# Block sums of the weights moved into attention chunks, a second pair with two levels in its first layer, rectifications on ScalarE and a padded state

## The chip, the cores and the metric

The kernel runs on one core of a Trainium2 chip. Its engines are TensorE (PE, with its weight load PEld), VectorE (DVE), ScalarE (ACT), GpSimd (POOL) and SyncE (SP), which issues most transfers. The metric is the device time of one execution in microseconds. A time before or after is the median of several executions. The profile is one further execution.

## The reference

The first half is linear attention with decay, for 4 batches, 8 heads, 768 positions and 64 columns per head. Positions go in blocks, and a 64x64 state per head carries the past:

```
intra = ((q_b k_b^T) * Dmask) v_b
inter = (q_b * lam_pow) kv_state
out_b = intra + inter
kv_state = lam_block * kv_state + (k_b * rev_pow)^T v_b
```

Its output, with the heads side by side, is x (4 batches x 768 x 512). The second half mixes x by a Fourier transform over positions and columns and adds a two-layer network:

```
u  = x + real(fft(fft(x, axis=1), axis=2))
un = (u - mean(u)) / sqrt(var(u) + 1e-6)
y  = u + max(un @ w_ch1, 0) @ w_ch2       # w_ch1: 512 x 2048, w_ch2: 2048 x 512
```

All of it is in float32. The two weights come in as 64-bit floats and are converted on the chip.

## The kernel before, in words

**Front.** Each batch b goes through six attention chunks of 128 positions. `attn_in` loads k, q and v of a chunk (L263, on SP's queue, two buffers each), multiplies k by the decay on GpSimd (L270), transposes k and q on TensorE (L274, L279) and copies them out on ScalarE (L276, L281). `attn_out` makes the scores (L298), scales them by the decay on VectorE (L302), makes the state's increment (L315), takes the state on (L319 on GpSimd multiplies by the decay, L320 on VectorE adds the increment), and then sums two products into one bank: the old state with the scaled queries (L328, one 64x64 product per head) and the scores with v (L332). ScalarE copies the result (L335), and TensorE turns it back (L348). State tiles alternate: `st[0]`, `st[1]`. Batch 0 keeps its mirrored rows on the chip (`TURNED`); the others send theirs through DRAM and gather them with GpSimd's indirect transfers (L439 to L452). After that comes the transform (`fft_ln`, L516 to L611) and the normalization.

Twelve groups of 256 rows come out, (b, g). The first four (`PLAIN`) go through the plain network `mlp` (L635 first layer, L649 second layer, rows stored from `y`, L660 to L661), in between the attention and transform work of later batches: `weave` and `beside` mix generators by planned costs, which each `yield` gives. The weights are loaded and converted between them (`load_weights`, L209 to L225; buffers tagged "e", two of them, which the transposed rows L576 use too).

**Late.** The other eight groups (`LATE`) are taken in four pairs of 2 x 256 rows. A pair's two layers are done by a fast matrix product with seven block products in place of eight (`PRODUCTS`). The second layer of every pair, and both layers of pairs 3 and 4, apply that twice (`deep_first`, L967; `deep_second`, L1037): 7 x 7 products of blocks with 128 moving columns. The first layer of pairs 1 and 2 applies it once (`first_layer`, L882): in eight steps i, each with 14 matmuls of 256 columns into three banks X, Y and Z. `DEEP = 2` says how many pairs do so. In a step TensorE writes and adds to bank X several times, and ScalarE reads X between (L904, L911, L914), so the next addition waits for that copy. VectorE adds Y or Z to what ScalarE has copied (L906, L894, L915) and rectifies it in place (L907, L895, L916); `finish` of a step, which runs in the next step, also rectifies X on ScalarE into `sv` (L892) and makes the sums L896 and L897.

Two levels need block sums of the weights (four sums for each of seven blocks of each weight). `keep_sums` (L714) makes those of the second weights during the first layer of pair 1, `keep_sums_w` (L731) those of the first weights during that of pair 2, both on GpSimd with tiles tagged "tx" (six buffers), and SP stores each in DRAM. Before a block product, three of them are loaded again (`load_three`, L755). The fourth is written over a quarter of the weight: by GpSimd in place for the second weights (L718), by a load for the first (`place_sums_w`, L741).

**What sets the order.** Each engine works through its own list in order. A scheduler that places instructions by planned costs makes the list from the program; instructions in `tc.keep_in_program_order` keep their place. SP's list holds stores and loads alike: each waits for its semaphore in its turn.

Of the kernel before, what the change touches and what calls it, by code (L numbers as in the profile page):

```python
# [10 lines left out]
F32 = mybir.dt.float32  # L11
# [65 lines left out]
def kernel(  # L77
# [97 lines left out]

    st = [const.tile([128, HP, D], F32, name=f"st{i}") for i in range(2)]

# [75 lines left out]

    ins, oTs, eo = {}, {}, {}
    LEADS = (0,)
# [3 lines left out]
    def attn_in(b, c):  # L259
# [13 lines left out]
        for hp in range(HP):  # L273
            nc.tensor.transpose(ptk[:, hp, :], pair(kt, hp), ident)  # L274
        kT = new(at, [128, HP, C], "kT", bufs=2)
        nc.scalar.copy(kT, ptk)  # L276
        ptq = psum_a([128, HP, C])
        for hp in range(HP):
            nc.tensor.transpose(ptq[:, hp, :], pair(qt, hp), ident)  # L279
        qT = new(at, [128, HP, C], "qT", bufs=2)  # L280
        nc.scalar.copy(qT, ptq)  # L281
# [7 lines left out]
    def attn_out(b, c, head):  # L289
# [14 lines left out]
        if last and b - 1 in LEADS:  # L304
            mirror_a(b, pin=True)
        yield 1.5


        s_old, s_new = st[(c + 1) % 2], st[c % 2]
        if not last:  # L310
            pu = psum_a([128, HP, D])
            for hp in range(HP):
                for hi in range(2):
                    h = 2 * hp + hi
                    mm(pu[HD[hi], hp, :], lhsT=kd[:, h, :], rhs=vt[:, h, :], start=True, stop=True)  # L315
            if c == 0:
                nc.vector.tensor_copy(s_new, pu)
            else:
                nc.gpsimd.tensor_tensor(s_new, s_old, spow.broadcast_to([128, HP, D]), op=ALU.mult)  # L319
                nc.vector.tensor_tensor(s_new, s_new, pu, op=ALU.add)  # L320
            yield 0.9


        po = psum_a([128, HP, C])
        if c > 0:
            for hp in range(HP):
                for hi in range(2):
                    mm(po[HD[hi], hp, :], lhsT=s_old[HD[hi], hp, :], rhs=qs[HD[hi], hp, :],  # L328
                       start=(hp == 0), stop=False, skip_group_check=True)
        for hp in range(HP):  # L330
            for hi in range(2):
                mm(po[HD[hi], hp, :], lhsT=vt[:, 2 * hp + hi, :], rhs=sc[hi][:, hp, :],  # L332
# [9 lines left out]
        yield 2.0  # L342
        yield from head

        def turn(oT):
# [364 lines left out]

    s2.td = []
    s2.begun = wt.tile([128, 1], F32, name="begun")

    def keep_sums(k):  # L714

        pin = tc.keep_in_program_order
        B11, B12, B21, B22 = quarters_b(s2.B[PRODUCTS[k][1]])
        pin(nc.gpsimd.tensor_tensor(B12, B22, B12, op=SUB))  # L718
        T1, T2, T4 = t = [new(s2.yp, [128, HF // 2, HM // 2], "tx", bufs=6) for _ in range(3)]
        s2.td.append([dram.tile([128, HF // 2, HM // 2], F32, name=f"td{k}{i}") for i in range(3)])  # L720
        for i, o, x, y, op in ((1, T2, B12, B11, ADD), (0, T1, B22, T2, SUB), (2, T4, B21, T2, SUB)):
            pin(nc.gpsimd.tensor_tensor(o, x, y, op=op))
            nc.sync.dma_start(s2.td[k][i], o)

    s2.sd = []

# [3 lines left out]

    def keep_sums_w(k):  # L731

        pin = tc.keep_in_program_order
        A11, A12, A21, A22 = quarters_w(s2.A[PRODUCTS[k][0]])
        S3, S2, S1, S4 = [new(s2.yp, [128, FH // 2], "tx", bufs=6) for _ in range(4)]
        s2.sd.append([dram.tile([128, FH // 2], F32, name=f"sd{k}{i}") for i in range(4)])
        for i, o, x, y, op in ((3, S3, A11, A21, SUB), (1, S2, A22, S3, SUB), (0, S1, S2, A11, ADD), (2, S4, A12, S2, SUB)):
            pin(nc.gpsimd.tensor_tensor(o, x, y, op=op))
            nc.sync.dma_start(s2.sd[k][i], o)

# [25 lines left out]
    PAIRS = len(LATE) // 2  # L766
    DEEP = 2
    pairs = [Pair() for _ in range(PAIRS)]
# [106 lines left out]
    def first_layer(j):  # L875
# [12 lines left out]
        def finish(i, X, Z):  # L888
# [5 lines left out]
            V.tensor_tensor(a12, two(Z), a12, op=ADD)  # L894
            V.tensor_scalar(a12, a12, 0.0, None, op0=ALU.max)  # L895
            V.tensor_tensor(s1, a21, a22, op=ADD)  # L896
# [3 lines left out]
        for i in range(HF):  # L900
# [5 lines left out]
            V.tensor_tensor(a11, two(Y), a11, op=ADD)  # L906
            V.tensor_scalar(a11, a11, 0.0, None, op0=ALU.max)  # L907
            if last:
# [6 lines left out]
            V.tensor_tensor(a22, two(Z), a22, op=ADD)  # L915
            V.tensor_scalar(a22, a22, 0.0, None, op0=ALU.max)  # L916
            last = (i, X, Z)
            if j < min(DEEP, 2) and i < len(PRODUCTS):
                if i == 0:
                    tc.keep_in_program_order(nc.gpsimd.tensor_copy(s2.begun, h["a11"][:, 0, 0, 0:1]))  # L920
                (keep_sums, keep_sums_w)[j](i)
            if i == HF - 3:
# [216 lines left out]
    def late():  # L1139
        for j in range(PAIRS):  # L1140
            if j < DEEP:
                open_pair(j)
                if j == 0:
                    run(inputs(0))
                first_layer(j)
                if j + 1 < DEEP:
                    in_step(second_layer(j) + [(inputs(j + 1), iter(()))])
        in_step(second_layer(DEEP - 1) + [w for j in range(DEEP, PAIRS) for w in deep_pair(j)])
# [31 lines left out]
    def run(gen):  # L1180
        return sum(gen)
# [82 lines left out]
```

## Time and profile before

| | us |
|---|---|
| median of 3 executions (796.07 to 801.15) | 797.12 |
| profiled execution | 798.86 |
| its span, first to last instruction | 796.9 |
| TensorE busy | 766.8 (96%) |
| VectorE busy | 587.7 (74%) |
| ScalarE busy | 216.7 (27%) |
| GpSimd busy | 195.6 (25%) |
| first layer of pair 1, L882 | 428.7 to 478.6 |
| first layer of pair 2, L882 | 521.7 to 570.8 |
| first layer of pair 3, L967, begins | 611.2 |

A line of the profile names the line of the kernel, the engine, the operation, and what is written from what with sizes and number. In a time line the first column is the start and the second the duration, in us from the start of the span; in brackets is the idle time ahead of the instruction and what ended it. "SPq" is a transfer issued by SP. Each matrix product in float32 appears as two matmuls. A matmul's duration is longer than its distance to the next, because they overlap; distances are what counts.

### The profile page before, as it was taken

The page shows a single profiled execution, that of the slowest core. Times are in us where ns is not written, and L with a number is a line of the kernel's source. Part 1 is how long each engine was busy: PE and PEld are TensorE (multiplying, and loading weights), DVE is VectorE, ACT ScalarE, POOL GpSimd, SP SyncE. Part 2 cuts the span into 40 slices and gives each one's busy share as a digit, 9 for nine tenths or more (in the row PEclk, how much of TensorE's full clock was granted, in tenths as well). Part 3 has the DMA queues.
Part 4 walks back from the last instruction along what each step waited for, and adds up shares of the span by engine and source line. Part 5 has one row for each costly group of instructions (what it writes and reads, how often), then busy time and mean ns, then how long its engine had stood idle before and what let it go on. Part 6 is the DMA issues. An engine that isn't in the chain of part 4 may idle for free.

```text
span 796.9 us, 14576 instructions
## 1 busy us (share of the span) xinstructions
PE 766.8 (96%) x5616; PEld 647.2 (81%) x5616; DVE 587.7 (74%) x1148; ACT 216.7 (27%) x512; POOL 195.6 (25%) x196
## 2 busy tenths in 40 slices
PE   6989999999999999999999999999999999999996
PEld 5768776858675766777956889998999999999995
DVE  6899889685853573246598998769977699758983
ACT  3755443324431221221200221012210442024300
POOL 3233231011101020121003960279204101230021
PEclk9999999999999999999999999999999999999999
DMA  9979624238842037443232375345954555455432
GB/s 241 260 152 253 179 84 130 92 58 215 206 131 87 27 79 144 103 132 106 47 71 89 138 239 170 95 167 190 326 170 145 165 175 178 129 177 187 125 121 79
DMA packets 152331, 116.80 MB, mean 147 GB/s; under 512 B 113998, under 2 KB 113998, under 8 KB 152262
## 3 DMA queue, kind: packets, MB, share of 16 engines
q1 hardware_dynamic: 147120, 103.39, 46.1%
q0 software_dynamic: 2112, 6.69, 2.5%
q10 hardware_dynamic: 3030, 5.78, 2.1%
q8 instruction: 45, 0.74, 0.4%
q14 instruction: 24, 0.20, 0.1%
HBM read 83.58 MB, written 32.25 MB: 145 GB/s over the span
## 4 chain that ended last, share of the span: by engine, by line
PE 77%; DVE 10%; DMA 6%; issue 4%; ACT 2%; POOL 1%; SPq 0%; POOLq 0%; ACTq 0%; DVEq 0%
PE p L1037 21%; PE p L882 12%; PE p L967 11%; PE pm L649 9%; PE pm L635 8%; PE pa L516 3%; PE pa L332 3%; PE pa L298 3%; DMA raw<-in_moe_w_ch_dram 2%; DMA x<-xb,ix 2%; PE pa L328 2%; PE pa L274 1%; PE pa L315 1%; PE pa L348 1%; PE pa L279 1%
## 5 line engine op out<-in xcount | busy, mean ns | idle before, releaser
L635 PE MATMUL pm<-ut,w 128*128 128x256 f32 x512 | 118.8, 381 | 0.0
L649 PE MATMUL pm<-w,hr 128*128 128x512 f32 x256 | 115.7, 596 | 0.1
L635 PEld LDWEIGHTS pm<-ut,w 128*128 128x128 f32 x512 | 94.5, 190 | 14.0 <-issue 2.1
L649 PEld LDWEIGHTS pm<-w,hr 128*128 128x128 f32 x256 | 46.6, 190 | 49.3 <-issue 48.0
L1051 POOL TENSOR_TENSOR y<-y,u 128x512 f32<-128x512 f32 x12 | 18.8, 1570 | 199.1 <-DVE y L1060 156.7
L1037 PE MATMUL p<-tx,sx 128*128 128x128 f32 x416 | 54.9, 275 | 0.0
L1037 PEld LDWEIGHTS p<-tx,sx 128*128 128x128 f32 x416 | 50.6, 192 | 0.0
L882 PE MATMUL p<-ur,w 128*128 128x256 f32 x192 | 46.9, 379 | 0.1
L270 POOL TENSOR_TENSOR kd<-k,decay 128x512 f32<-128x512 f32 x20 | 22.2, 1109 | 95.9 <-PE pa L315 58.0
L1045 DVE TENSOR_TENSOR y<-p,y 128x128 f32<-128x128 f32 x92 | 25.6, 286 | 22.4 <-PE p L1037 15.7
L1043 ACT COPY y<-p 128x128 f32<-128x128 f32 x48 | 12.8, 266 | 104.1 <-PE p L1037 103.8
L882 PEld LDWEIGHTS p<-ur,w 128*128 128x128 f32 x192 | 36.3, 190 | 5.7 <-issue 0.5
L302 DVE TENSOR_TENSOR sc<-pa,decay 128x512 f32<-128x512 f32 x48 | 31.5, 683 | 8.5 <-PE pa L298 8.2
L1037 PE MATMUL p<-w,ha 128*128 128x128 f32 x288 | 37.4, 275 | 0.0
L298 PEld LDWEIGHTS pa<-qT,kT 64*128 64x128 f32 x384 | 26.0, 193 | 13.2 <-ACT qT L281 7.2
L1037 PEld LDWEIGHTS p<-w,ha 128*128 128x128 f32 x288 | 35.0, 192 | 0.2
L332 PE MATMUL pa<-sc,v 128*64 128x128 f32 x384 | 31.5, 282 | 3.8 <-DVE sc L302 3.7
L643 ACT ACTIVATE hr<-pm 128x256 f32<-128x256 f32 x44 | 16.7, 384 | 65.9 <-PE pm L635 65.6
L298 PE MATMUL pa<-qT,kT 64*128 64x128 f32 x384 | 30.7, 292 | 3.2 <-ACT qT L281 2.9
L549 POOL TENSOR_SCALAR ve<-mv 128x2 f32<-128x2 f32 x12 | 3.4, 286 | 122.6 <-DVE mv L546 122.6
L882 PE MATMUL p<-sx,w1s 128*128 128x256 f32 x128 | 32.9, 380 | 0.2 <-DVE sx L785 0.2
L332 PEld LDWEIGHTS pa<-sc,v 128*64 128x64 f32 x384 | 23.1, 137 | 11.4 <-DVE sc L302 5.3
(227 smaller groups left out, 1717.4 us busy)
## 6 DMA issues: line engine op xcount, KB each, us to landing
tx<-td SPq DMA_DIRECT2D x84, 256.0 KB, 2.9
raw<-in_moe_w_ch_dram SPq DMA_DIRECT2D x32, 512.0 KB, 5.4
tx<-sd SPq DMA_DIRECT2D x42, 256.0 KB, 2.7
sd<-tx SPq DMA_DIRECT2D x28, 256.0 KB, 2.0
k<-in_k_dram SPq DMA_DIRECT2D x24, 256.0 KB, 5.0
q<-in_q_dram SPq DMA_DIRECT2D x24, 256.0 KB, 6.0
v<-in_v_dram SPq DMA_DIRECT2D x24, 256.0 KB, 4.4
td<-tx SPq DMA_DIRECT2D x21, 256.0 KB, 2.0
```

Of the source, the lines that this page charges most:

```text
L270: nc.gpsimd.tensor_tensor(kd, kt, kpow, op=ALU.mult)
L298: mm(pss[hi][:, hp, :], lhsT=kT[HD[hi], hp, :], rhs=qT[HD[hi], hp, :], start=True, stop=True)
L302: nc.vector.tensor_tensor(t, pss[hi], decay[:, hi::2, :], op=ALU.mult)
L332: mm(po[HD[hi], hp, :], lhsT=vt[:, 2 * hp + hi, :], rhs=sc[hi][:, hp, :], start=(c == 0 and hp == 0), stop=(hp == HP - 1), skip_group_chec ...
L516: mm = nc.tensor.matmul(ps[:, n, :], lhsT=piece(a, i, n), rhs=cs[0:rows, a, i in (2, 3), n, :], start=(a == 0), stop=(a == 1))
L635: nc.tensor.matmul(ps, lhsT=w1[:, c, 128 * fc:128 * fc + 128], rhs=ut[:, c, :], start=(c == 0), stop=(c == KO - 1))
L649: nc.tensor.matmul(ps, lhsT=hr[(fc - f0) // 4][:, fc % 4, 128 * i:128 * i + 128], rhs=w2[:, fc, :], start=(fc == f0), stop=(fc == f1 - 1))
L882: nc.tensor.matmul(ps, lhsT=s2.A[a][:, kt, 128 * i:128 * i + 128], rhs=U[b][:, kt, :], start=(first and kt == 0), stop=(kt == 1), skip_gro ...
L967: nc.tensor.matmul(ps[:, 128 * i:128 * i + 128], lhsT=ab[m][0][:, 128 * i:128 * i + 128], rhs=ab[m][1], start=(start and i == 0), stop=Tru ...
L1037: nc.tensor.matmul(ps[:, 0:HM // 2], lhsT=ab[m][0][i], rhs=ab[m][1][:, i, :], start=(start and i == 0), stop=(i == HF // 2 - 1), skip_grou ...
L1045: V.tensor_tensor(o, ps[:, 0:HM // 2], o, op=ADD)
L1051: nc.gpsimd.tensor_tensor(o, y, u, op=ADD)
```

## The change

- The first layer of pair 2 has two levels like pairs 3 and 4 (`DEEP = 1`), so only pair 1 uses `first_layer`.
- Block sums of six weight blocks (24 sums) are made on GpSimd in the first four attention chunks of batches 2 and 3, three in each, in buffers "e" and a new one "ss". Each is stored by SP. The remaining 32 are made during the first layer of pair 1, and three quarters of the second weights are loaded back at its start (`place_sums_b`).
- In that layer the three rectifications after VectorE's additions are made by ScalarE.
- In batches 2 and 3 ("padded") the state is updated in place in one tile, and ScalarE copies it into a tile with zeros in the other head's rows; L328 multiplies all 128 rows. The increment, state and score products follow each other without a point at which other work may be put between. Zeros are set at each batch's start.
- `kT` and `qT` have one buffer in place of two.

```diff
-    st = [const.tile([128, HP, D], F32, name=f"st{i}") for i in range(2)]
+    st = const.tile([128, HP, D], F32, name="st")
+    sd = const.tile([128, HP, 2, D], F32, name="sd")
+    turns_of = [st, sd[:, 0:HP // 2].rearrange("p h a d -> p (h a) d")]
...
-        kT = new(at, [128, HP, C], "kT", bufs=2)
+        kT = new(at, [128, HP, C], "kT")
...
-        yield 1.5
-        s_old, s_new = st[(c + 1) % 2], st[c % 2]
+        padded = b not in TURNED and b - 1 not in LEADS
+        yield 2.4 if padded and not last else 1.5
+        s_old, s_new = (st, st) if padded else (turns_of[(c + 1) % 2], turns_of[c % 2])
+        if padded and c == 0:
+            nc.gpsimd.memset(sd, 0.0)
...
-            yield 0.9
+            if not padded:
+                yield 0.9
...
-                    mm(po[HD[hi], hp, :], lhsT=s_old[HD[hi], hp, :], rhs=qs[HD[hi], hp, :],
-                       start=(hp == 0), stop=False, skip_group_check=True)
+                    old, qh = (sd[:, hp, hi, :], qs[:, hp, :]) if padded else (s_old[HD[hi], hp, :], qs[HD[hi], hp, :])
+                    mm(po[HD[hi], hp, :], lhsT=old, rhs=qh, start=(hp == 0), stop=False, skip_group_check=True)
+        if padded and not last:
+            for hi in range(2):
+                nc.scalar.copy(sd[HD[hi], :, hi, :], st[HD[hi]])
         for hp in range(HP):
-            for hi in range(2):
+            for hi in (1, 0) if padded else (0, 1):
...
         yield from head
+        if padded and c < 4:
+            if not sums:
+                sums.append(early_sums())
+            run(part(sums[0], 3.0))
...
-    def keep_sums(k):
-    def keep_sums_w(k):
+    def block_sums(layer, k, quarters, shape, stage):
+        Q11, Q12, Q21, Q22 = quarters
+        S3, S2, S1, S4 = [stage[i](shape) if callable(stage[i]) else stage[i] for i in range(4)]
+        d = (s2.sd, s2.td)[layer][k] = [dram.tile(shape, F32, name=f"{'st'[layer]}d{k}{i}") for i in range(4)]
+        if layer == 0:
+            todo = ((3, S3, Q11, Q21, SUB), (1, S2, Q22, S3, SUB), (0, S1, S2, Q11, ADD), (2, S4, Q12, S2, SUB))
+        else:
+            todo = ((3, S3, Q22, Q12, SUB), (1, S2, S3, Q11, ADD), (0, S1, Q22, S2, SUB), (2, S4, Q21, S2, SUB))
+        for i, o, x, y, op in todo:
+            tc.keep_in_program_order(nc.gpsimd.tensor_tensor(o, x, y, op=op))
+            if o is not Q12:
+                nc.sync.dma_start(d[i], o)
+            yield 1.0
+    def early_sums():
+        k1, k2, f1, f2 = slice(0, 2), slice(2, 4), slice(0, FH), slice(FH, DFF)
+        b1, b2, c1, c2 = slice(0, HF), slice(HF, FO), slice(0, HM), slice(HM, DM)
+        blocks = [(0, 0, w1[:, k1, f1]), (1, 0, w2[:, b1, c1]), (0, 1, w1[:, k2, f1]), (1, 1, w2[:, b2, c1]),
+                  (0, 5, w1[:, k2, f2]), (1, 6, w2[:, b2, c2])]
+        for layer, k, t in blocks:
+            for d in block_sums(layer, k, (quarters_w, quarters_b)[layer](t), SHAPES[layer],
+                                [lambda s: new(ep, s, "e")] + [ep.tile(SHAPES[layer], F32, tag="ss", bufs=1, name=f"ss{layer}{k}")]
+                                + 2 * [lambda s: new(ep, s, "e")]):
+                yield d
+    def later_sums(i):
+        for layer, k in (((1, 3),), ((1, 2),), ((1, 4),), ((1, 5),), ((0, 3),), ((0, 4),), ((0, 2), (0, 6)))[i]:
+            q = (quarters_w, quarters_b)[layer]((s2.A, s2.B)[layer][PRODUCTS[k][layer]])
+            run(block_sums(layer, k, q, SHAPES[layer], [q[1] if layer else stage_tx] + 3 * [stage_tx]))
+    def place_sums_b():
+        for k in (0, 1, 6):
+            nc.sync.dma_start(quarters_b(s2.B[PRODUCTS[k][1]])[1], s2.td[k][3])
...
-    DEEP = 2
+    DEEP = 1
...
-            V.tensor_scalar(a12, a12, 0.0, None, op0=ALU.max)
+            nc.scalar.activation(a12, a12, AF.Relu)
...
-            V.tensor_scalar(a11, a11, 0.0, None, op0=ALU.max)
+            nc.scalar.activation(a11, a11, AF.Relu)
...
-            V.tensor_scalar(a22, a22, 0.0, None, op0=ALU.max)
+            nc.scalar.activation(a22, a22, AF.Relu)
...
-                (keep_sums, keep_sums_w)[j](i)
+                later_sums(i)
...
     def late():
-        for j in range(PAIRS):
-            if j < DEEP:
-                open_pair(j)
-                if j == 0:
-                    run(inputs(0))
-                first_layer(j)
-                if j + 1 < DEEP:
-                    in_step(second_layer(j) + [(inputs(j + 1), iter(()))])
+        open_pair(0)
+        run(inputs(0))
+        first_layer(0)
         in_step(second_layer(DEEP - 1) + [w for j in range(DEEP, PAIRS) for w in deep_pair(j)])
```

## The prediction

> **What bounds the kernel now.** I read the page first, busy shares and the 40 slices, then the chain that ended last, then the time line of the three stages that the diff touches.
>
> ```profile
> PE 766.8 (96%) x5616; PEld 647.2 (81%) x5616; DVE 587.7 (74%) x1148; ACT 216.7 (27%) x512; POOL 195.6 (25%) x196
> PE   6989999999999999999999999999999999999996
> PE 77%; DVE 10%; DMA 6%; issue 4%; ACT 2%; POOL 1%; SPq 0%; POOLq 0%; ACTq 0%; DVEq 0%
> ```
>
> TensorE is the bound from the third slice to the end, at full clock. The reader is to see what follows: matmul time taken out anywhere after about 60 us comes off the end, and so does any new wait of TensorE count in full. GpSimd and ScalarE have three quarters of the span free, but on average only; what matters is who waits for them in the two places where they get work.
>
> The first place is the first pair's first layer (428.7 to 478.6 us), one of its eight steps:
>
> ```profile
> 452.09 2.61 POOL L722 TENSOR_TENSOR tx<-w2s,tx 128x512 f32<-128x512 f32 x2
> ...
> 453.67 1.03 PE L882 MATMUL p<-ur,w1s 128*128 128x256 f32 x4
> 453.94 0.91 DVE L916 TENSOR_SCALAR ha<-ha 128x256 f32<-128x256 f32 x1
> 454.53 1.03 PE L882 MATMUL p<-sx,w 128*128 128x256 f32 x4
> ...
> 454.78 0.38 ACT L892 ACTIVATE sv<-p 128x256 f32<-128x256 f32 x1 [1.40 <-PE p L882]
> ...
> 456.06 0.41 DVE L896 TENSOR_TENSOR hs<-sv,ha 128x256 f32<-128x256 f32 x1
> ...
> 456.39 1.48 DVE L897 TENSOR_TENSOR hs<-ha,sv 128x256 f32<-128x256 f32 x1
> 456.46 0.37 ACT L911 COPY ha<-p 128x256 f32<-128x256 f32 x1 [1.29 <-PE p L882]
> ...
> 457.12 1.03 PE L882 MATMUL p<-sx,w1s 128*128 128x256 f32 x4
> ...
> 457.80 0.41 DVE L894 TENSOR_TENSOR ha<-p,ha 128x256 f32<-128x256 f32 x1
> ```
>
> Groups of four matmuls follow each other every 0.864 us without a gap. The group at 457.12 may start only after the copy L911 has read the bank, and L911 starts 0.2 us after its matmuls because ScalarE has nothing in front of it. VectorE is behind (L894 is 2.4 us after its matmuls), but nobody on TensorE waits for it. L897 takes 1.48 us here and 0.42 us once GpSimd is idle.
>
> The second place is the queue that loads attention chunks of batch 3:
>
> ```profile
> 312.34 0.39 SPq L263 DMA_DIRECT2D k<-in_k_dram  x1
> ...
> 315.02 0.85 SPq L263 DMA_DIRECT2D k<-in_k_dram  x1
> ...
> 329.95 0.37 SPq L263 DMA_DIRECT2D k<-in_k_dram  x1
> 330.66 0.37 SPq L263 DMA_DIRECT2D q<-in_q_dram  x1
> 335.72 0.37 SPq L263 DMA_DIRECT2D v<-in_v_dram  x1
> 336.33 0.38 SPq L263 DMA_DIRECT2D k<-in_k_dram  x1
> ```
>
> These are keys of chunks 2, 3, 4 and 5; their transposes run at 328.7, 335.6, 341.7 and 347.8 us, so each load is 11 to 20 us ahead, of which 4 are the transfer. Chunks follow every 6.07 us there.
>
> [...] The trace shows 0.17 us of idle weight load ahead of L332 after L328 and again after L332. [...]
>
> **The change, part by part.** The sum is made against the profiled execution (798.86 us, span 796.9, so about 2.0 around it); it is 1.7 above the median of 797.12, and I apply the difference to the median.
>
> *Second pair's first layer two-level.* Removed: 7 products x 8 x 2 = 112 matmuls, 224 in the trace, at 0.864/4 = 0.216 us: 48.4 us (521.67 to 570.75 less 0.67 us of second layer). Added: 7 x 7 x 4 = 196, 392 in the trace. In the later pairs eight take 0.893 us (784 in 611.17 to 698.72), so 43.8 us. **-4.6 us** on TensorE. The VectorE and GpSimd work that comes with it, and 21 loads of 256 KB more, are what pairs 3 and 4 have now behind an unbroken TensorE; the DMA share there is 0.45 to 0.6. I cost it at nothing, 0 to +3 if the loads of sums, the seven replaced quarters and the next inputs (34 loads of 256 KB and two of 512 KB in 44 us, some 220 GB/s, against 390 seen at 570 us) come late.
>
> *Padded state, batches 2 and 3.* The eight L328 matmuls of a chunk become 128 rows deep with 64 columns, as L332's. L332's sixteen take 1.03 us, L328's 1.02: no price in themselves. Two changes of mode per chunk go (state update to L328, L328 to L332), 0.17 us each at most, in 10 chunks, and where matmuls of the MLP now stand between the state update and L328 or inside L332 (six places) one interruption of 0.2 us. Between 0 and 3.4 + 1.2 = 4.6; I take **-3 us**. The ScalarE copies into the padded tile (20 of 64x256, some 0.38 us by L352) are queued ahead of the copy of the output, behind VectorE's state sum; a next use is 5 us later, so nothing.
>
> *24 sums in attention.* Three per chunk in four chunks of both batches, 128x512, 1.06 us by L270 alone, 1.3 with VectorE beside them, in GpSimd's order ahead of some key products (L270) and state products (L319); and 24 stores on SP's queue, each of which waits for its sum, ahead of the k, q and v loads of the next chunks. Two sums share two buffers with the weight conversion, so stores must land (2.0 us) before reuse.
> Batch 3: the order puts a sum behind the indirect output store, which starts at 327.74 now (VectorE's y). Then: three sums to 332, key product, key load of chunk 3 issued at 332.5 instead of 315, lands 336.5, its use is at 337.5 (more MLP is ordered ahead): just hidden. Key product 3 to 337.6, two sums to 340.2, key load 4 issued 340.5, lands 344.5 against 344.2; the query load is one sum later, 346.4 against 344.9: 1.5 us. Key product 4 to 345.6, three sums to 349.5, key load 5 lands 353.8 against 351.9: 2 us. With 4.4 us for a load, as the median is over both batches, some **+5 us** (0 where the loads land in 3.2 us and VectorE's y comes earlier; +10 where the two batches' chunks go at 9 instead of 6 us).
> Batch 2: chunks are 9 to 17 us apart, and the loads keep 1 to 3 us of their slack: **+1** (0 to +5).
>
> *Sums in the first pair's first layer.* 32 instead of 28, at 38.75/28 = 1.38 us: GpSimd is busy until 477.4 instead of 471.8. Three quarters of the second weights come back by loads at the layer's start, for products 45 us later. The second layer's loads follow the last sums; nothing, unless that layer starts on time (then +1).
>
> *Rectifications on ScalarE.* 24 leave VectorE (0.91 us each with GpSimd beside it), which is not waited for: no gain. [...] In its order the rectification of a12 of step i-1 stands **ahead of** the copy L911 of step i, and it waits for the VectorE sum L894, which stands behind L896 and L897. So TensorE's 457.12 group now waits for: end of s4 group (0), L892 to 0.63, L896 from 0.67 with a mean wait of half a GpSimd sum (0.65) and 0.41, L897 1.40 more (it meets the next sum), L894 0.34, rectification 0.45, copy and handover 0.36: 4.3 us, where three groups give 2.59. **1.7 us per step** (1.0 to 2.4). Steps become 7.75 us; from 436.4 on, 5.5 of seven meet GpSimd: 9.4, and 0.16 to 0.5 in the rest where the splits come in: **+10 us**. Bounds: 0 if VectorE gets in between sums, 14.
>
> Sum: -4.6 - 3 + 5 + 1 + 10 = +8.4; span 805.3, profiled 807.3, median **805.5 us**.
>
> **Rivals.**
> 1. *The rectification chain does not hold TensorE* (not slower). Place: ScalarE's copy L911. It decides from L896 and L897 together below 1.1 us after L892; uncontended they take 0.8. Against it: 1.48 for L897 in nearly all of the 16 steps. Then +8.4 - 10 = -1.6: 795.5; with the attention loads hidden too, -7.6: 789.5.
> 2. *The loads in attention stay hidden*: for it, GpSimd is a quarter busy; against it, stores with waits stand ahead of the loads in one queue. +2.4: 799.5.
> 3. *The queue locks both batches*: conversion buffers, stores and loads wait for each other in batch 2 as well, 2 to 3 us in each of eight chunks, some +18 in place of +6: 817.
> That the two-level layer isn't faster can't be: both prices are in the trace.
>
> **How the numbers follow.** The forecast (800 to 811) 0.50, of which a bit over half is slower by over 1% (8 us, about what a measurement of this kernel can tell from no change); rival 1 alone 0.16 and with both gains 0.08; rival 2 0.11; rival 3 0.15. Slower 0.29 + 0.15 = 0.44, and 0.02 of mixed cases; faster the 0.07 of rival 1 with both; the rest within. Below rival 1's 795.5 less 1 and above 816 some 0.2 is left out: range 794 to 816.
>
> **What would show it.** Second pair's first layer about 43.8 us with eight matmuls in 0.89; no 0.17 us ahead of L332; in the first layer a wait of TensorE on ScalarE's copy of 1 to 2.4 us per step, 60 instead of 50 us long; waits on k and q loads at chunks 4 and 5 of batch 3. Wrong, if TensorE stays unbroken in the first layer, or if the waits sit in batch 2.

## The result, and the profile after

The changed kernel takes **809.64 us** (median of 6, 808.42 to 812.46) where the kernel before takes 797.05 us on the same chip: a ratio of **1.0142 (95% interval 1.0119 to 1.0164)**, slower. (The quotient of the two medians alone is 1.0158.) The prediction was 805.5 us. The profiled execution took 812.46 us, its span 810.3 us (before: 798.86 and 796.9). It is the slowest of its six, 2.8 us above their median; that of before is 1.8 above its own.

Cut at the same instructions, the two profiles part as follows (us; "start" is the first key transpose of batch 2, L274 before and L276 after; "first layer" is that of pair 1, L882 and L915):

| | before | after | difference |
|---|---|---|---|
| up to the start of batch 2 | 161.0 | 162.6 | +1.6 |
| batches 2 and 3, with the transform behind them | 267.7 | 276.7 | +9.0 |
| first layer of pair 1 | 50.0 | 59.0 | +9.0 |
| from there to the last matmul | 310.4 | 305.7 | -4.6 |
| last matmul to end of span | 7.8 | 6.3 | -1.5 |

Four profiles have the code of the changed kernel up to the first layer (its own, and three of the runs below). Batch 2 takes 129.7 to 130.5 us in them and batch 3, with its transform, 143.7 to 146.2. The changed kernel's own profile has the largest value of both, so differences in attention are known to 1 us or 2.5 us, not to a tenth.

From the page of the changed kernel, the busy shares and TensorE's slices:

```profile
PE 764.4 (94%) x5784; PEld 649.2 (80%) x5784; DVE 569.0 (70%) x1115; ACT 240.0 (30%) x556; POOL 200.3 (25%) x207
...
PE   6888999999799999988999889999999999999996
```

TensorE still is the bound, but it is no longer unbroken. A slice is 20.3 us. Behind the first four slices, a 7 stands at 203 to 223 us, 8s at 344 to 385 and at 446 to 486, where 9s stood before: the attention of batches 2 and 3 and the first layer. What TensorE waited for (line, what released it: sum, times, longest):

```profile
PE p L915 <- ACT ha L944: 7.5, 5, 1.7
PE pa L281 <- DMA q<-in_q_dram: 5.9, 2, 3.6
PE pa L276 <- DMA k<-in_k_dram: 5.8, 2, 4.9
...
PE pa L529 <- DVE fe L488: 3.2, 2, 2.2
```

The first two rows are new. (4.9 us of the third are at the program's start and were there before.) The 2.2 us of the last row are at 380.04, in the transform of batch 3, where no single wait of that line was over 1.5 us before.

One step of the first layer after, as a time line (start, duration, in brackets the idle time ahead and its end). L929, L930, L927 and L944 are the lines that were L896, L897, L894 and L911; L928 is the rectification of a12:

```profile
454.35 0.38 ACT L925 ACTIVATE sv<-p 128x256 f32<-128x256 f32 x1
...
454.77 1.29 DVE L929 TENSOR_TENSOR hs<-sv,ha 128x256 f32<-128x256 f32 x1 [0.78 <-ACT sv L925]
...
455.98 1.48 DVE L930 TENSOR_TENSOR hs<-ha,sv 128x256 f32<-128x256 f32 x1
...
457.38 0.41 DVE L927 TENSOR_TENSOR ha<-p,ha 128x256 f32<-128x256 f32 x1
457.83 0.42 ACT L928 ACTIVATE ha<-ha 128x256 f32<-128x256 f32 x1 [3.10 <-DVE ha L927]
458.15 0.35 ACT L944 COPY ha<-p 128x256 f32<-128x256 f32 x1
458.56 1.13 PE L915 MATMUL p<-sx,w1s 128*128 128x256 f32 x4 [1.66 <-ACT ha L944]
```

It is the chain that the prediction named: ScalarE stands 3.10 us in front of L928, which waits for the two contended sums L929 and L930 and for L927; the copy L944 stands behind it, and TensorE behind the copy. The same wait comes again at 466.52, 474.48 and 482.44, so a step takes 7.96 us, where seven groups of 0.864 us are 6.05. A first, shorter one (0.85 us) stands at 450.59.

The two sums are long beside GpSimd. Before, L897 (here L930) took 1.48 or 1.49 us in the twelve of its 16 steps in which a sum of GpSimd ran beside it, and ended 0.28 or 0.29 us after the end of such a sum each time; in the four without it took 0.42 us. Here it takes 1.48 or 1.49 us in five of eight steps and 0.42 in three. VectorE's rectifications took 0.91 us in most steps beside the sums and 0.29 or 0.30 without; L894, which has one input from a bank, took 0.41 or 0.42 in all 16.

The load of the second place, chunk 4 of batch 3, in time order:

```profile
347.50 0.32 SPq L743 DMA_DIRECT2D td<-e  x1
...
347.91 0.40 SPq L265 DMA_DIRECT2D q<-in_q_dram  x1
...
352.75 0.65 PE L281 MATMUL pa<-ident,q 128*128 128x128 f32 x4 [2.27 <-DMA q<-in_q_dram]
```

The store of a block sum goes out at 347.50, as soon as GpSimd has made the sum, the query load right behind it at 347.91, although the buffer it fills was last read by the transposes of chunk 2, which end at 338.30; its transposes wait 2.27 us for it. In batch 2 the same happens to chunk 4, and longer:

```profile
213.78 1.52 POOL L741 TENSOR_TENSOR e<-w 128x512 f32<-128x512 f32 x1 [1.91 <-DMA td<-e]
...
215.33 0.32 SPq L743 DMA_DIRECT2D sd<-e  x1
...
215.74 1.51 SPq L265 DMA_DIRECT2D q<-in_q_dram  x1
...
220.19 1.08 PE L281 MATMUL pa<-ident,q 128*128 128x128 f32 x4 [3.62 <-DMA q<-in_q_dram]
```

GpSimd stands 1.91 us until an earlier sum has left the buffer "e" for DRAM, then makes the next sum; its store waits for that, and the query load waits behind the store. TensorE stands 3.62 us, its longest wait behind the program's start.

### The profile page after: what moved, and what is told of

Same layout as the page of the kernel before. It is cut to its first block, busy times and chain, and to the rows that moved or that the text cites. A ratio compares the mean times of both kernels' runs of the same rounds, so it can differ in the third digit from the quotient of the medians.

```text
span 810.3 us, 15048 instructions
## 1 busy us (share of the span) xinstructions
PE 764.4 (94%) x5784; PEld 649.2 (80%) x5784; DVE 569.0 (70%) x1115; ACT 240.0 (30%) x556; POOL 200.3 (25%) x207
## 4 chain that ended last, share of the span: by engine, by line
PE 76%; DVE 10%; DMA 6%; issue 4%; ACT 2%; POOL 1%; SPq 0%; POOLq 0%; DVEq 0%; ACTq 0%
PE p L1071 21%; PE p L1001 16%; PE pm L662 12%; PE pm L648 8%; PE p L915 4%; PE pa L529 3%; PE pa L300 2%; PE pa L341 2%; DMA raw<-in_moe_w_ch_dram 2%; PE pa L335 1%; DMA k<-in_k_dram 1%; DMA q<-in_q_dram 1%; PE pa L320 1%; PE pa L276 1%; PE pa L361 1%
## 5 line engine op out<-in xcount | busy, mean ns | idle before, releaser
L662 PE MATMUL pm<-w,hr 128*128 128x512 f32 x256 | 118.1, 605 | 0.0
L1071 PE MATMUL p<-tx,sx 128*128 128x128 f32 x400 | 52.8, 275 | 0.0
L1071 PEld LDWEIGHTS p<-tx,sx 128*128 128x128 f32 x400 | 48.7, 192 | 0.0
L1010 DVE TENSOR_TENSOR ha<-p,ha 128x512 f32<-128x512 f32 x60 | 40.1, 685 | 9.7 <-PE p L1001 9.5
L304 DVE TENSOR_TENSOR sc<-pa,decay 128x512 f32<-128x512 f32 x48 | 31.4, 683 | 10.6 <-PE pa L300 10.6
L300 PEld LDWEIGHTS pa<-qT,kT 64*128 64x128 f32 x384 | 26.5, 195 | 14.1 <-ACT qT L283 7.4
L1010 DVE TENSOR_TENSOR hs<-p,hs 128x512 f32<-128x512 f32 x39 | 26.2, 684 | 14.9 <-PE p L1001 14.9
L341 PE MATMUL pa<-sc,v 128*64 128x128 f32 x384 | 29.9, 279 | 5.0 <-DVE sc L304 4.9
L1001 PE MATMUL p<-sx,tx 128*128 128x128 f32 x264 | 33.9, 275 | 0.0
L287 DVE TENSOR_TENSOR qs<-pa,qpow 128x512 f32<-128x512 f32 x20 | 13.7, 686 | 27.5 <-ACT qT L283 27.4
```

Of the source, the lines that this page charges most:

```text
L300: mm(pss[hi][:, hp, :], lhsT=kT[HD[hi], hp, :], rhs=qT[HD[hi], hp, :], start=True, stop=True)
L304: nc.vector.tensor_tensor(t, pss[hi], decay[:, hi::2, :], op=ALU.mult)
L662: nc.tensor.matmul(ps, lhsT=hr[(fc - f0) // 4][:, fc % 4, 128 * i:128 * i + 128], rhs=w2[:, fc, :], start=(fc == f0), stop=(fc == f1 - 1))
L1001: nc.tensor.matmul(ps[:, 128 * i:128 * i + 128], lhsT=ab[m][0][:, 128 * i:128 * i + 128], rhs=ab[m][1], start=(start and i == 0), stop=Tru ...
L1010: V.tensor_tensor(o, p, o, op=ADD)
L1071: nc.tensor.matmul(ps[:, 0:HM // 2], lhsT=ab[m][0][i], rhs=ab[m][1][:, i, :], start=(start and i == 0), stop=(i == HF // 2 - 1), skip_grou ...
```

## The experiments

Each ratio below is against the kernel before, run on the same chip beside it. "Start" is the start of the first layer of pair 1 in that run's profile (before 428.7, after 439.3); "layer" its length (50.0, 59.0); "rest" the time from there to the last matmul (310.4, 305.7).

### All three rectifications back on VectorE

```diff
-            nc.scalar.activation(a12, a12, AF.Relu)
+            V.tensor_scalar(a12, a12, 0.0, None, op0=ALU.max)
```

and the same for a11 and a22.

> The three rectifications of the first pair's first layer go back to VectorE, all else as changed. Theory (on ScalarE the rectification of a12 stands ahead of the copy that frees bank X, and so holds TensorE): the layer falls from 58.8 to about 50 us, and the time from 809.6 to about 800.7 us. [...]

Measured: ratio 1.0085 (1.006 to 1.0111), layer 53.2, rest 307.4. The five waits on ScalarE are gone, so the chain is confirmed, but only 5.8 of the 9.0 us came back, and behind the layer 1.7 of them are lost again. What TensorE waits for in that stage, and two stretches of 10 us (stretch, its length, then busy time of PE, PEld, DVE, ACT, POOL, each with its number of instructions, TensorE's clock, DMA share, GB/s):

```profile
PE p L915 <- DVE ha L948: 2.9, 1, 2.9
...
480.00:490.00 10.00, 7.13 (x36) 6.06 (x35) 9.86 (x16) 1.58 (x5) 6.40 (x5) 1.00 0.71 258
490.00:500.00 10.00, 10.00 (x76) 9.95 (x75) 8.63 (x18) 1.33 (x5) 0.00 (x0) 0.83 0.99 370
```

With 32 sums of GpSimd beside it and its own rectifications, VectorE is busy 9.8 of 10 us from 450 to 490 and falls behind. At the layer's last step TensorE waits for it for 2.9 us, and then runs at half the clock for 3.4 us (0.83 in the mean of the second stretch), which makes the rest 1.7 us longer. So VectorE was not as free as its share of the span looked. In the kernel before it was as busy from 440 to 470 us, also 9.8 of 10, and TensorE never waited for it. That the four sums more are the difference is likely, since they keep GpSimd at work for longer, but no run changes their number alone.

### The rectification of a12 later in ScalarE's order

```diff
-            nc.scalar.activation(a12, a12, AF.Relu)
+            due.append(a12)
...
-            nc.scalar.copy(a12, two(X))
+            tc.keep_in_program_order(nc.scalar.copy(a12, two(X)))
...
             nc.scalar.copy(a22, two(X))
+            while due:
+                t = due.pop()
+                tc.keep_in_program_order(nc.scalar.activation(t, t, AF.Relu))
...
```

> All three rectifications stay on ScalarE; only that of a12 is placed behind the two copies of bank X of the next step. Theory (place in ScalarE's order): as good as all three back on VectorE, layer 50 to 52 us, time 800.5 to 803. Rival (ScalarE's added work, some 0.4 us for each of 24, is what counts, wherever it stands): layer 56 us or more, time 807 or more.

Measured: ratio 1.0071 (1.0047 to 1.0096); layer 51.6, rest 306.2. The step as a time line:

```profile
456.49 1.03 PE L915 MATMUL p<-ur,w 128*128 128x256 f32 x4
456.69 0.37 ACT L944 COPY ha<-p 128x256 f32<-128x256 f32 x1 [1.34 <-PE p L915]
...
457.35 1.03 PE L915 MATMUL p<-sx,w1s 128*128 128x256 f32 x4
...
458.69 0.42 ACT L950 ACTIVATE ha<-ha 128x256 f32<-128x256 f32 x1
```

Groups follow each other every 0.86 us again, the copy comes 0.2 us after its matmuls begin, and the rectification (here L950) behind it. So the place in the order is the cause, not the amount of work: 7.4 of the 9.0 us come back with all 24 rectifications still on ScalarE. One wait of 1.3 us for VectorE at the layer's end is left. The time can't be set against the layer to the microsecond, since attention, with the same code, ended at 435.0 here and at 439.3 in the changed kernel's profile; of that scatter more below.

### The 32 sums of that layer left out

> All as changed, but the 32 sums in the first layer of pair 1 are left out (early ones stand in for them, so the later products use other data). Theory (the rectification of a12 is late because VectorE's two-SBUF-input sums wait for GpSimd's): the layer takes 50.5 to 52 us with waits of at most 0.2 us per step, and the time is about 802. Rival (the place in ScalarE's order holds TensorE also with GpSimd idle): 56 us or more, 807 or more.

Measured: ratio 1.0046 (1.003 to 1.0061); layer 50.2, rest 305.7. With GpSimd idle the two sums take 0.42 us each in the mean, and the same order costs nothing: the wait needs both, the place in front of the copy and the contention that makes L929 and L930 late.

### The 24 sums in attention left out

> The 24 block sums in the attention chunks and their stores are left out (one stored tile stands in for them, so the later products use other data). Theory (these sums with their stores cost what attention lost): the first layer of pair 1 starts at about 427 us in place of 439, which is 1.7 before the kernel before (padded state -3, +1.2 that was lost ahead of batch 2), and the time is about 797.5. Rival (the padded state or the single buffers of the transposed keys and queries cost it): the start stays above 434 and the time above 804.

Measured: ratio 0.9984 (0.9966 to 1.0002); start 424.9, 14.4 us earlier than after. From the start of batch 2 to that of batch 3 it takes 123.3 us (after 130.5, so 7.2 for the sums), and from there to the first layer 139.3 (after 146.2, so 6.9). The theory holds, with both batches paying (against all four profiles with the sums, 6.3 to 7.2 us in batch 2 and 4.5 to 6.9 in batch 3).

### The 24 sums made, but not stored

> The 24 sums are made in the attention chunks as in the changed kernel, but not stored (one stored tile stands in for them). Theory (stores that wait in SP's order hold the loads behind them): most of it comes back, start of the first layer 428 to 430, time 798 to 801. Rival (GpSimd's own time delays the key products and state products): start above 436, time above 806.

Measured: ratio 1.0029 (0.9999 to 1.006); start 429.7. Neither was quite right, and the batches differ: batch 3 takes 139.2 us, as without the sums, so there the stores are everything. Batch 2 takes 128.9: of its 7.2 us only 1.6 went with the stores, and **5.5 us stay with the sums alone**. In batch 2 VectorE converts weights. Its group that differs most (198 to 236 us: group, count, sum in us, mean in ns, idle before), without the sums:

```profile
L224 DVE TENSOR_SCALAR w<-raw 128x512 uint32<-128x512 uint32 x6 | 2.5, 418 | 0.0
```

and with the sums, unstored; below it the wait that follows, from the time line:

```profile
L224 DVE TENSOR_SCALAR w<-raw 128x512 uint32<-128x512 uint32 x7 | 7.2, 1042 | 0.0
```

```profile
230.70 1.98 PE L335 MATMUL pa<-qs,sd 128*64 128x128 f32 x16 [2.69 <-DVE sc L304]
```

The same instruction takes 418 ns in the mean without GpSimd's sums and 1042 ns among them: 0.42 us at 222.91 and at 226.69, where GpSimd is idle, and 1.29 in the mean of the other five. VectorE is 9.9 of 10 us busy from 200 to 220 us (8.0 without the sums), then waits 2.28 us for a load of weights at 226.34, reaches the score products L304 late, and TensorE waits 2.69 us for them.

This is not the wait that the changed kernel itself has. There, in the same stretch, L224 takes 421 ns in the mean, VectorE is 6 to 7 of 10 us busy from 200 to 220 us, and TensorE waits for the query load (3.62 us), not for the scores. So batch 2 has two limits of nearly the same length, one over the other: loads behind waiting stores, and, with those gone, VectorE beside the sums. Taking one away shows the other.

The longer L224 is like L930 of the first layer beside GpSimd's sums (1.48 against 0.42 us); this run shows its length, not what makes it longer.

### The stores issued by GpSimd

```diff
-                nc.sync.dma_start(d[i], o)
+                (queue or nc.sync).dma_start(d[i], o)     # queue: nc.gpsimd for the early sums
```

> The 24 sums stay in the attention chunks, and their stores are issued by GpSimd behind each sum, not by SP. Theory (what costs is that a waiting store holds the loads behind it in SP's order): as without stores, the first layer starts near 430 and the time is 800 to 802. Rival (landing of stores and the two buffers cost it, or the issue on GpSimd at about 1 us each costs as much): start 435 or later, time 806 or more.

Measured: ratio 1.023 (1.019 to 1.027); start 445.6, worse than after. No load is late now, but in batch 2 (time line):

```profile
219.01 0.94 DVE L219 TENSOR_SCALAR e<-raw 128x512 uint16<-128x512 uint16 x1 [8.21 <-DMA td<-e]
...
220.60 1.97 PE L341 MATMUL pa<-sc,v 128*64 128x128 f32 x16 [5.41 <-DVE sc L304]
```

VectorE stands 8.21 us in front of a weight conversion, since the buffer "e" that it needs still has a sum in it whose store has not landed; the score product is queued behind that conversion. The granted clock was 0.5 from 219.13 to 229.37 on top of that. So the two shared buffers are a further lock. In the changed kernel it is there too: VectorE stood only 0.8 us for a store of "e" from 198 to 236 us, but GpSimd stood 1.91 us and ScalarE's conversion (L218) 6.22 us until one had landed, at 213.78 and 214.95, just ahead of the query load that came late. The rival named the landing and the buffers; the issue itself took GpSimd 0.56 to 0.67 us for each store of batch 2.

### Loads of k, q and v issued by ScalarE in batches 2 and 3, with the a12 rectification later

```diff
-            nc.sync.dma_start(t, src[b, :, rows, :].rearrange("h p d -> p h d"))
+            (nc.scalar if b > 1 else nc.sync).dma_start(t, src[b, :, rows, :].rearrange("h p d -> p h d"))
```

> In batches 2 and 3 the loads of k, q and v are issued by ScalarE, so that no store stands ahead of them; the 24 sums and their stores stay in the attention chunks and on SP; and the rectification of a12 stands behind the two copies. Theory (the queue): attention as without stores, first layer from about 430 us and 51.6 us long, time 792 to 794, faster than the kernel before. Rival (ScalarE's waits for free load buffers hold its own copies and so TensorE, as GpSimd's issue of the stores did): first layer from 437 or later, time 800 or more.

Measured: ratio 0.9991 (0.9978 to 1.0004); start 433.3, layer 51.6, so neither forecast was met. Batch 3 takes 139.6 us with all sums and stores in it, as without them: **in batch 3 the whole loss is loads behind waiting stores**. The wait at 380.04 in its transform is gone as well, here and without the stores; how it hangs on the loads was not traced. Batch 2 takes 130.8, no better than after: now VectorE's late score products hold TensorE, once for 3.5 us, as they did without the stores, and the granted clock is 0.5 for 6.8 us around that wait. VectorE is late there by the sums beside it and by the buffers "e", for which it stood 4.5 us from 198 to 236 us.

### The sums moved to the transform stages, with the a12 rectification later

```diff
-        if padded and c < 4:
...
+            if b > 1 and i < 4:                  # behind each of four products of the transform
+                if not sums:
+                    sums.append(early_sums())
+                run(part(sums[0], 3.0))
```

> The 24 sums leave the attention chunks for the transform stages of batches 2 and 3 (three at each of four of its products), where no key or query load comes behind their stores soon; and the rectification of a12 stands behind the two copies, as in the run before. Theory (both losses come from places in orders, not from the amount of work): first layer from about 426 us (the run without the sums had 424.9) and 51.6 us long, the rest 306: time about 791, some 8 below the kernel before. Rival (24 sums of 1.3 us cost VectorE's two-input operations as much wherever they are): the layer starts at 432 or later, time 797 or more.

Measured: ratio 1.028 (1.0247 to 1.0313); start 452.0, the worst of all. What TensorE waited for:

```profile
PE pa L525 <- DVE fe L484: 16.1, 4, 6.5
PE pa L525 <- DVE fe L479: 4.9, 1, 4.9
```

21 us, all of them on VectorE's folding of the rows, whose sums have two SBUF inputs each and are a chain that TensorE waits for. One of its steps, ahead of GpSimd's sums and among them:

```profile
257.48 0.42 DVE L484 TENSOR_TENSOR fe<-fe 128x256 f32<-128x256 f32 x1
...
381.16 1.51 DVE L484 TENSOR_TENSOR fe<-fe 128x256 f32<-128x256 f32 x1
```

From L435 to L484 the chain took 3.3 us the first time and 10.1 the second. Beside the waits, the granted clock was 0.5 for 30.7 us of these two batches (17.1 from 269.97, 6.8 from 379.20, 6.8 from 392.85), so some of the loss is slower matmuls. The theory "place in orders, not amount of work" fell here: attention's chunks did run without a wait of over 1.0 us, but among the sums the folding, which TensorE needs next, took 10.1 us in place of 3.3.

### The padded state undone, without the early sums

> Without the 24 early sums (one stored tile stands in for them) and with the state as in the kernel before: 64x64 products of the old state, two state tiles. Against the run without the sums alone (first layer from 424.9, 797.5). Theory (changes of tiling mode cost 0.17 us each): start 428, time about 800.5. Rival (no gain in the padded state, or a loss by the copies into it): start 425 or earlier, time 797 or less.

Measured: ratio 1.0047 (1.0028 to 1.0067); start 428.2. Batches 2 and 3 take 266.7 us, against 262.6 with the padded state: **-4.1 us** for it, 2.3 in batch 2 and 1.8 in batch 3. The 0.17 us of idle weight load ahead of the products with v (L332 before, L341 after) is gone, as forecast.

### The kernel before with the padded state alone, and with single buffers alone

> The kernel before with the padded state alone (with the single buffers of the transposed keys and queries, whose room the padded state takes). Theory (3.3 us gained in batches 2 and 3, some 1.2 lost ahead of batch 2 by the single buffers): 795 us where the kernel before has 797, first layer of pair 1 from 426.6. Rival (the gain holds only with the changed order of the rest): 797 or more.

Measured: ratio **0.993 (0.9908 to 0.9952)**; start 423.3, rest 310.4. Batches 2 and 3 take 262.7 us. It is faster than both kernels, if by less than 1% than the one before.

> The kernel before with one buffer in place of two for the transposed keys and queries. Theory (this is what the changed kernel lost ahead of batch 2): chunk 3 of batch 0 starts near 28.5 us in place of 26.6, and chunk 1 of batch 2 at 176.6 in place of 175.5. Rival (other differences): 26.6 and 175.5 as before.

Measured in one profile: batch 2 starts at 161.00 us and its chunk 1 at 175.49, to the digit what the kernel before has, and batches 2 and 3 take 266.7 us (before 267.7). Chunk 3 of batch 0 starts at 27.7 us, between the 28.5 of the theory and the 26.6 of before; in the kernel with the padded state, which has the single buffers too, it starts at 26.6. So no cost of the single buffers is left by batch 2, and the +1.6 us of the changed kernel are mostly scatter: the eleven profiles with its code, nearly alike up to there, begin batch 2 between 160.4 and 163.4. Their mean is 161.8 and that of the three profiles with the code of before 160.9, so a part below 1 us may be the change's; no run shows what.

### The changed kernel with three orders altered

```diff
-        if padded and c < 4:
-            run(part(sums[0], 3.0))
+        if padded and (c < 4 if b == 3 else c > 3):
+            run(part(sums[0], 3.0 if b == 3 else 6.0))
```

with the loads of batch 3 on ScalarE and the a12 rectification behind the copies.

> The changed kernel with three orders altered: 12 of the 24 sums are made at the end of chunks 4 and 5 of batch 2, where VectorE has four fifths of its time free until 256 us, the other 12 at chunks 0 to 3 of batch 3; the loads of k, q and v of batch 3 are issued by ScalarE; the rectification of a12 stands behind the two copies. Theory (what the sums cost is VectorE's work beside them and the loads behind their stores): first layer from 425 to 427 us and 51.6 us long, time 790 to 792. Rival (the gathers of batch 2, which now stand behind six sums in GpSimd's order, or the two buffers of the sums, hold TensorE): first layer from 431 or later, time 796 or more.

Measured: 791.4 us, ratio **0.9899 (0.988 to 0.9918)**; start 425.4, layer 51.6, rest 306.8. Batch 2 takes 124.5 us and batch 3 139.6, against 123.3 and 139.3 without the sums. Its longest waits in sum:

```profile
PE pa L276 <- DMA k<-in_k_dram: 5.0, 1, 5.0
PE pa L581 <- DVE un L576: 3.4, 4, 1.0
PE pa L341 <- DVE sc L304: 3.3, 7, 1.2
```

The same work as in the changed kernel in 2.4% less time by the two ratios, and in a span of 790.1 in place of 810.3 us: no query load and no copy L944 is waited for, and none of the waits behind 60 us is over 1.4 us. The 5.0 us are those of the program's start. The granted clock stays full from 60 us to the last matmuls. The three edits were not run one by one in this form.

## Why the prediction was right and wrong

Its side and its sign were those of the forecast (slower, +8.4 us against +12.6 in the medians). By its steps, with the sizes that the runs gave:

| step of the sum | put at | measured | from |
|---|---|---|---|
| second pair's first layer two-level | -4.6 | -4.6 | rest, 310.4 to 305.7 |
| padded state | -3 | -4.1 | with and without it |
| 24 sums, batch 3 | +5 | +6.9 (4.5 to 6.9) | with and without them |
| 24 sums, batch 2 | +1 | +7.2 (6.3 to 7.2) | with and without them |
| rectifications on ScalarE | +10 | +9.0 | layer, 50.0 to 59.0 |

The padded state and the sums together make +10.0 of the +9.0 that attention lost; the kernel without either takes 1.0 less there than before. With the +1.6 ahead of batch 2, mostly scatter, and the -1.5 behind the last matmul, the span's +13.4 is accounted for within a tenth. The -1.5 is no scatter: that end takes 7.8 to 8.1 us in the three kernels with the code of before and 6.2 to 6.9 in all eleven with that of the change. The prediction has no such term, and no run shows which part of the change it comes from.

- **Two-level layer**: right to the tenth; the cover named (VectorE, GpSimd and the loads of sums) held, as TensorE is unbroken from 500 us on.
- **Padded state**: right in sign, 1.1 us too small. Where nothing is put between, from the state update to the next transposes, a chunk is only 0.19 us shorter in batch 3 (2.47 against 2.66 us), some 2 us in ten chunks. Another 0.46 us is a shorter wait for the scores of batch 3's first chunk (1.24 against 1.70). The rest of the 4.1 may lie in how the other work falls between the products, which no run separates. No run shows a price of 0.17 us for a change of mode, as it was put at most: without the two changes L335 begins 0.09 us and L341 0.10 us sooner behind the products ahead of them, which are those 0.19 us.
- **Sums in batch 3**: the mechanism was right (a load behind waiting stores in SP's order; loads by ScalarE take it away whole), and the size within the bounds given. The wait sat at chunk 4's query load, as worked out; that of chunk 5's key load did not come in this profile (1.03 us in the one with the rectifications on VectorE). The second wait of the batch, 2.24 us for the folding in its transform, was not foreseen.
- **Sums in batch 2**: this is the step that failed, and it makes up more than the whole miss. It counted only loads that keep 1 to 3 us of their slack. Chunk 4's query load kept none and held TensorE for 3.62 us, with half the clock for 3.41 us behind it; the prediction's own sign of being wrong, waits in batch 2, came with it. The way there is a lock: a sum waits for a buffer "e" whose store has not landed, the next store waits for the sum, and the load stands behind that store. Under it lies a second limit that the step didn't ask for: VectorE's weight conversions beside GpSimd's sums (L224 1042 ns with the sums unstored, 418 without them) and the score products behind them, although the step on the rectifications counts with the like (L897 1.48 against 0.42 us), VectorE converts the weights there and the page of before shows it 8 tenths busy in the slices from 159 and from 199 us. It shows once the stores are gone (5.5 of the 7.2 us stay) or the loads are moved (130.8 us, with VectorE held by the buffers as well). Because either limit alone holds TensorE nearly as long, their shares don't add up, and 7.2 us is the price of both. With the sums made in chunks 4 and 5, stores and loads of batch 2 still in SP's list, batch 2 takes 124.5 us: the place, not the number of the sums, sets the price.
- **Rectifications**: the chain, its links and its lines came as written; the order in it is ScalarE's. No run shows two of its terms, the 0.45 us for a rectification and the mean wait of half a sum ahead of L896: L928 took 0.42 us in all eight steps, and L929, with 1.06 us put for it and its wait, took 1.22 to 1.29 in the four that TensorE waited for in full. The total is near in part by luck: a step lost 1.91 us (7.96 against 6.05) where 1.7 was put, but TensorE waited in only four steps and, half as long, in a fifth, where 5.5 were put. Wrong is a remark beside it, that taking 24 rectifications from VectorE is "no gain", since VectorE "is not waited for". Put back, they leave 4.9 us of loss (3.2 in the layer and 1.7 behind it), since VectorE then ends the layer late. Both directions of such a move have a price; here the move pays with the rectification of a12 one place later (layer and rest 51.6 and 306.2 us, against 53.2 and 307.4 with all three on VectorE).
- **Rivals**: the third (both batches lock, +18 in place of +6) was about as near in size as the forecast: +11.0 to +14.1 in the four profiles with the sums. Its mechanism, conversion buffers and stores and loads that wait for each other, is what the trace shows ahead of the wait at 220.19. It isn't 2 to 3 us in each of eight chunks, though, but one long wait in each batch, with what follows from it, and it leaves out VectorE. The first is refuted by the time line, the second by the waits on query loads.

## What to carry to other kernels

Ask of every step given to an idle engine what its busy share doesn't answer: what stands behind it, and behind the stores of its results, in an engine's list, and who waits for that; and which work of VectorE runs beside it if the engine is GpSimd (here a sum of two inputs took 1.48 us beside it and 0.42 without). Work moved to a stage is free only if these are clear there. The same 24 sums cost 1.5 us in one place, with the loads of one batch on another queue, and 29 in another, half clock included (264.1 and 291.6 us for batches 2 and 3 in the last run and in that with the transform, against 262.6 without sums). When one wait is taken away and the time hardly moves, look for the next one under it before calling the first harmless. When a bet has several parts, time the parts alone: here one of them was worth 0.7% by itself.

## What was not expected of the hardware

**TensorE's granted clock fell to half for 3.4 us or more around some waits, and it mattered where a wait fell.** Three stretches of the changed kernel around the query wait that ends at 352.75 (the number before the last two is the granted clock):

```profile
349.82:353.23 3.41, 1.15 (x11) 0.93 (x10) 0.00 (x0) 1.27 (x3) 3.33 (x4) 1.00 0.96 240
353.23:356.64 3.41, 3.41 (x14) 1.91 (x14) 0.69 (x1) 1.23 (x3) 1.33 (x2) 0.50 0.69 208
356.64:360.05 3.41, 3.41 (x64) 2.99 (x61) 1.61 (x3) 0.87 (x3) 0.00 (x0) 1.00 1.20 293
```

So this wait of 2.27 us cost, by an estimate from these figures (half of 3.41), about 1.7 us more. In the fourteen profiles, from 60 us on, 17 of 21 waits of 1.8 us or more had such a fall around them or within 1.3 us behind them, and none of the twenty waits of 1.64 to 1.66 us behind the copy of bank X (L944 in the changed kernel).

What decided in these profiles can be read from the starts of the falls. In every profile with several of them they lie whole multiples of 3.413 us apart; in the changed kernel they are 220.11, 353.23 and 380.53, which is 39 and 8 times that. Cut each profile, from 60 us to its last matmuls, into windows of this length on its own grid: TensorE stood 1.9 us or more in 15 windows that began at full clock, and all 15 were followed by half the clock. Of all windows with less, three were (1.81, 1.61 and 1.22 us). So a wait of 3.59 us at 219.33 in the run with the rectifications on VectorE went unpunished: it lies across two windows, with 1.74 and 1.85 us in each. A fall lasted one window in most cases, and at most five (17.1 us in the run with the sums in the transform).

Three of these falls are in the changed kernel's attention and transform, by the same estimate some 5 of the us that it lost there, and as kernels with the same code up to the first layer had one, two and three of them, they are part of the scatter of 435.0 to 439.3 us in its start.
